# Attention weights turned by two DMA transposes, with the taps laid in another order in PSUM and a new order of issue

## The chip, the cores and the metric

The kernel runs on one core of a Trainium2 chip. The metric is the device time of one execution in microseconds (us), and lower is better. A core has five engines with instruction streams of their own: TensorE (PE in the profile; its weight loads are listed apart as PEld), VectorE (DVE), ScalarE (ACT), GpSimd (POOL) and SyncE (SP), which here only issues DMAs. Matrix products go to PSUM, a small accumulator memory, and are copied from there to SBUF, the main on-chip memory, by DVE or ACT.

## What is computed

Two independent layers on inputs of 2048 positions by 448 features, whose outputs stand side by side in the result. Cut to what matters:

```python
# A: a diagonal state space model with complex state of 448
h = Lam_bar * h + Bu[:, t]                     # for each t of 2048
y = 2.0 * einsum("blp,dp->bld", hseq, Cmat).real + x * Dskip

# B: attention of each position to 8 earlier ones, 2 apart
H, Dh, W, dil = 16, 28, 8, 2
idx = pos[:, None] - (arange(W) * dil)[None, :]
logits = einsum("bhsd,bhswd->bhsw", q, k[idx]) * Dh ** -0.5
logits = where(idx >= 0, logits, -1e9)
attn = softmax(logits, axis=-1)                # over the W = 8 taps
o = einsum("bhsw,bhswd->bhsd", attn, v[idx])
out_b = o.reshape(B, S, D) @ wo

out = concatenate([y, out_b], axis=-1)
```

All inputs and outputs are bf16.

## The kernel before, in words

**Layout.** The 2048 positions are 128 chunks of 16: position = 16 * chunk + j. Keys, queries and values are made for one j at a time, so a tap (2 positions back) is mostly another j of the same chunk, and only the first few j reach into the chunk before, for which small halo copies exist. Attention is worked in two halves, b = 1 (j from 8 to 15) first, then b = 0. In a half, 8 positions j are split as r (2 runs) and i (4 within a run).

**Attention up to the weights (class PartB).** `prep` (L411) makes queries and keys on PE, four chunks' columns at a time (L476, L483, L509), and ACT or DVE copies them out of PSUM. `qk` (L579) multiplies queries and keys of a pair of taps on DVE (L649, L651, L655) into one of three product buffers; `summ` sums the products over Dh on PE (L666, L672) into the PSUM tile `logits` of 128 partitions (i, r, head) by 8 taps by 128 chunks. `softmax` (L689), once for each half, is a chain over engines: the mask is added on PE (`mask`, in `consts2`, L247), DVE takes the maximum over taps (`top`, L695), PE subtracts it (`sub`, L699), ACT takes the exponential (`exp`), PE sums over taps (`tot`, L710), DVE normalizes (`norm`, L714 and L716) into `attn_t`. Now the weights stand as (i, r, head) by chunk, while the values stand by chunk on partitions. So `tr` (L722) turns the eight 128x128 blocks on PE into a PSUM tile, and `ev` (L727) copies them in two pieces on ACT to the tile `attn`, whose free dimensions there are ordered so that two taps of a pair lie next to each other.

**The weighted sum.** `pv` (L788) multiplies weights by values on DVE (`mul`, L817: 3584 elements on each of 128 partitions, two taps at a time, 16 times in all) and adds them (L820, L829, L832). Half and run go in the order (b, r) = (1,1), (1,0), (0,1), (0,0). For three of these four groups the result is turned by a DMA transpose on SP (`trd`, L857); for the last one PE turns it (L869) and ACT copies it (L874). PE multiplies by the output weights (L885, L893, L900), and the result is copied out (L214, L218) and stored by SP (L910).

**The state space model (class PartA)** is interleaved with it: small parameters (L1092 to L1103) and powers of the state matrix (L1182) on DVE, the scan and its products on PE (L1232 to L1339), outputs on PE (L1430, L1434), copied or added (L1446) and stored (L1449). SP loads x by DMA transposes (L979), C by eight DMAs (L1005), and turns C by one more (L1009).

**What sets the order.** Every piece of work is a unit given to `Planner.add` (L115) with its engine (or two to choose from), a planned cost, its dependencies and the buffers that it takes and gives back. `Planner.run` (L129) issues the units in the order of the hand-over list `ORDER` if its length is that of the list of units, which is so here; a number from 1000 on means the unit's second engine (for evictions, DVE in place of ACT). Each engine then does its own instructions in that order, and waits are set by what each reads and writes. All DMAs of SP use eight semaphores in turn, so a DMA waits until the eighth one before it has landed. PSUM tiles come from small pools: the tag "W" has one slot (the logits), "s" six, which `tr`, `tot`, the output products and others share; there are three product buffers.

Of the kernel before, what the change touches and what calls it, by code (L numbers as in the profile page):

```python
# [18 lines left out]
NCH = 128  # L19
# [185 lines left out]
class Ctx:  # L205
# [41 lines left out]
    def consts2(self):  # L247
# [22 lines left out]
        def masks():  # L270
            G.memset(mrow[:], 0.0)
            G.affine_select(out=mrow[:], in_=mrow[:], compare_op=ALU.not_equal, fill=-1e9,
                            base=-3, pattern=[[1, 4]], channel_multiplier=1)
            G.memset(mcol[:], 1.0)
            for b in range(2):
                for k in range(2):
                    v = mcol[:, b, k].rearrange("p (i r h) -> p i r h", i=4, r=2)
                    G.affine_select(out=v, in_=v, compare_op=ALU.is_ge, fill=0.0, base=8 * k - 8 * b - 1,
                                    pattern=[[-1, 4], [-4, 2], [0, H]], channel_multiplier=2)
# [36 lines left out]
class PartB:  # L316
# [262 lines left out]
    def qk(self, b, prio):  # L579
# [8 lines left out]
        for g in (2 * b + 1, 2 * b):  # L588
            par = g - 2 * b
            j0 = 4 * g  # L590
            for tp in (3, 2, 1, 0):
# [65 lines left out]
                def summ(g=g, tp=tp, par=par, ub=ub, head=first):  # L657
# [5 lines left out]
                    zs = slice(H - H * par, 3 * H - H * par)  # L663
                    for kt in range(3):
                        for i in range(4):
                            nc.tensor.matmul(lg[32 * i:32 * i + 32, 2 * tp:2 * tp + 2, :],  # L666
                                             lhsT=cx.Z[:, kt, zs], rhs=pr[:, :, i, kt, :],
                                             start=(new and kt == 0), stop=(kt == 2), skip_group_check=True)
                    if tp < 2:
                        for z, t2 in ((cx.Z[:, 3, zs], tp + 2), (cx.Zh[:, zs], tp)):  # L670
                            for i in range(4):
                                nc.tensor.matmul(lg[32 * i:32 * i + 32, 2 * t2:2 * t2 + 2, :],  # L672
                                                 lhsT=z, rhs=ub["p3"][:, :, i, 0, :],
                                                 start=False, stop=True, skip_group_check=True)
# [14 lines left out]
    def softmax(self, b, prio):  # L689
# [29 lines left out]
        def tr():  # L719
            pt = box["pt"] = self.psum.tile([NCH, W, 2, 4, H], bf16, name="pt_at", tag="s")  # L720
            for w in range(W):
                nc.tensor.transpose(pt[:, w].rearrange("q r i h -> q i r h"), box["a"][:, w, :], cx.ident[:])  # L722

        def ev():
            at = self.attn[b] = pool.tile([NCH, W // 2, 2, 2, 4, H], bf16, name="attn%d" % b)
            for x in range(2):
                nc.scalar.copy(at[:, 2 * x:2 * x + 2].rearrange("q z r y i h -> q y (z r) (i h)"),  # L727
                               box["pt"][:, 4 * x:4 * x + 4].rearrange("q (y z) r i h -> q y (z r) (i h)", y=2))
# [6 lines left out]
        u = P.add("PE", pe(8, 128), tr, [u], -1, acq="s", rel="at")  # L735
        self.u_attn[b] = P.add("ACT", 2 * act(512), ev, [u], -1, rel="s")
# [51 lines left out]
    def pv(self, b, prio, deps):  # L788
# [13 lines left out]
        for r in (1, 0):  # L802
            last = getattr(self, "pv_last", None)
            us = (5, 4, 1, 0)
            for n in range(4):

                def step(n=n, r=r, part=0):
# [4 lines left out]
                    def mul(i):  # L812
                        u = us[i]
                        o = j0 + 4 * r + DIL * u
                        aa = self.attn[b][:, 2 * (u // 4) + u % 2, r].rearrange("q y i h -> q (y i) h").unsqueeze(2).to_broadcast(
# [755 lines left out]
```

## Time and profile before

| | before |
|---|---|
| median of 3 runs | 140.28 us |
| lowest and highest run | 140.21 and 141.18 us |
| span of the profiled execution | 138.7 us |
| median less that span | 1.58 us |
| granted TensorE clock | full speed in all 40 slices |
| instructions in the profile | 2854 |
| SP's DMA queue: share of 16 engines' time | 54.0% |

How to read it: the span is the time from the first to the last instruction of one profiled execution; what lies around it is in the median and not in the profile, so a forecast on the span has 1.58 us added. The page gives for each engine its busy time and share, then the chain that ended last (each piece is followed back to what released it). A timeline row gives the start in us, the busy time of a group of like instructions, the engine, the line of the code, the operation, what it writes and reads, and in square brackets how long the engine had been idle and what released it. "x3" at its end is a count. A row on "SPq" is the time that SP takes to issue a DMA; the landing is given apart, from the start of the issue. Since instructions of an engine overlap a little, the next start can lie before the last end, and the pitch of like instructions is shorter than the busy time of one.

### The profile page before, as it was taken

The page shows a single profiled execution, that of the slowest core. Times are in us where ns is not written, and L with a number is a line of the kernel's source. Part 1 is how long each engine was busy: PE and PEld are TensorE (multiplying, and loading weights), DVE is VectorE, ACT ScalarE, POOL GpSimd, SP SyncE. Part 2 cuts the span into 40 slices and gives each one's busy share as a digit, 9 for nine tenths or more (in the row PEclk, how much of TensorE's full clock was granted, in tenths as well). Part 3 has the DMA queues.
Part 4 walks back from the last instruction along what each step waited for, and adds up shares of the span by engine and source line. Part 5 has one row for each costly group of instructions (what it writes and reads, how often), then busy time and mean ns, then how long its engine had stood idle before and what let it go on. Part 6 is the DMA issues. An engine that isn't in the chain of part 4 may idle for free.

```text
span 138.7 us, 2854 instructions
## 1 busy us (share of the span) xinstructions
PE 131.6 (95%) x1078; PEld 68.5 (49%) x1085; DVE 123.8 (89%) x136; ACT 90.0 (65%) x202; POOL 17.7 (13%) x69
## 2 busy tenths in 40 slices
PE   5999999999999999999999999999999999988990
PEld 1634435444555554756435564545655554534640
DVE  2268999899999999999999999999999999999820
ACT  3464589997563967776685998987637070722671
POOL 7489820028000000000000000000000000000000
PEclk9999999999999999999999999999999999999999
DMA  4979943645653349735898019000000827965774
GB/s 128 266 128 213 173 87 63 160 101 116 80 111 74 82 84 145 140 81 150 230 185 195 0 25 112 0 0 2 5 0 0 183 82 43 213 211 155 234 233 139
DMA packets 39582, 16.05 MB, mean 116 GB/s; under 512 B 31573, under 2 KB 38932, under 8 KB 39569
## 3 DMA queue, kind: packets, MB, share of 16 engines
q1 hardware_dynamic: 39506, 15.87, 54.0%
q8 instruction: 8, 0.13, 0.4%
q14 instruction: 5, 0.04, 0.1%
q10 hardware_dynamic: 63, 0.01, 0.0%
HBM read 4.32 MB, written 3.67 MB: 58 GB/s over the span
## 4 chain that ended last, share of the span: by engine, by line
DVE 35%; PE 31%; SPq 15%; issue 7%; DMA 6%; ACT 3%; DVEq 0%; ACTq 0%
DVE rb L820 13%; DVE prods L817 11%; SPq L361 8%; PE v_ps L762 7%; DVE rb L817 4%; PE qk_ps L476 4%; DMA out_dram<-qk 3%; PE logits L666 3%; PE y_ps L1434 3%; DMA rb<-in_B_x_dram 3%; DVE pw L1182 2%; DVE rb L829 2%; PE wo_ps L900 2%; PE scb L1232 2%; PE scp L1232 2%
## 5 line engine op out<-in xcount | busy, mean ns | idle before, releaser
L817 DVE TENSOR_TENSOR prods<-attn,vd 128x3584 bf16<-128x3584 bf16 x12 | 24.1, 2019 | 0.0
L820 DVE TENSOR_TENSOR rb<-rb,prods 128x3584 bf16<-128x3584 bf16 x11 | 22.2, 2021 | 0.1
L651 DVE TENSOR_TENSOR prods<-qk 128x3072 bf16<-128x3072 bf16 (+1 forms) x15 | 19.1, 1327 | 0.0
L214 ACT CAST qk<-wo_ps 128x448 bf16<-128x448 f32 (+1 forms) x16 | 8.3, 527 | 12.2 <-PE wo_ps L893 7.7
L1434 PE MATMUL y_ps<-Ccat,qk 128*128 128x448 bf16 x60 | 15.1, 352 | 0.1
L476 PE MATMUL qk_ps<-rb 128*128 128x512 bf16 x60 | 14.4, 379 | 0.0
L1434 PE MATMUL y_ps<-Ccat,h 128*128 128x448 bf16 x45 | 11.0, 352 | 0.9 <-ACT qk L214 0.9
L214 ACT CAST vd<-v_ps 128x448 bf16<-128x448 f32 x15 | 7.4, 539 | 5.8 <-PE v_ps L762 4.5
L1232 PE MATMUL scb<-xaT_sb,Bcat 128*128 128x512 bf16 x42 | 10.9, 380 | 0.0
L1232 PEld LDWEIGHTS <-Bcat 128*128 128x128 bf16 x84 | 7.6, 100 | 6.6 <-issue 0.4
L1284 ACT CAST ubuf<-scb 128x64 bf16<-128x64 f32 x35 | 7.1, 218 | 5.6 <-PE scb L1291 3.5
L762 PE MATMUL v_ps<-rb 128*128 128x448 bf16 x48 | 9.9, 353 | 0.0
L655 DVE TENSOR_TENSOR prods<-qk 128x768 bf16<-128x768 bf16 (+3 forms) x18 | 9.1, 569 | 0.3 <-ACT qk L214 0.2
L216 ACT ACTIVATE qk<-qk_ps 64x512 bf16<-64x512 f32 (+1 forms) x15 | 8.9, 599 | 0.6 <-PE qk_ps L509 0.3
L476 PEld LDWEIGHTS <-rb 128*128 128x128 bf16 x60 | 5.6, 98 | 7.1 <-DMA rb<-in_B_wqkv_dram 0.5
L1434 PEld LDWEIGHTS <-qk 128*128 128x128 bf16 x60 | 5.9, 98 | 5.3
L817 DVE TENSOR_TENSOR rb<-attn,vd 128x3584 bf16<-128x3584 bf16 x4 | 8.1, 2022 | 0.1
L893 PE MATMUL wo_ps<-wo_p,rb 128*128 128x448 bf16 x36 | 8.1, 354 | 0.0
L1182 DVE TENSOR_TENSOR pw<-Dm,spair 128x1920 bf16<-128x1920 bf16 x7 | 8.1, 1153 | 0.0
L214 ACT CAST qk<-qk_ps 128x512 bf16<-128x512 f32 (+2 forms) x11 | 6.3, 585 | 2.6 <-PE qk_ps L483 1.1
L1232 PE MATMUL scp<-xaT_sb,Bcat 128*128 128x512 bf16 x30 | 7.8, 380 | 0.0
L666 PE MATMUL logits<-prods,Zsel 128*32 128x256 bf16 x192 | 7.4, 274 | 0.0
(199 smaller groups left out, 261.9 us busy)
## 6 DMA issues: line engine op xcount, KB each, us to landing
out_dram<-qk SPq DMA_DIRECT2D x32, 112.0 KB, 1.8
vd<-vd SPq DMA_DIRECT2D x3, 392.0 KB, 4.7
rb<-in_B_wqkv_dram SPq DMA_DIRECT2D x3, 336.0 KB, 5.0
qk<-in_A_x_dram SPq DMA_DIRECT2D x1, 448.0 KB
ra<-in_A_B_re_dram SPq DMA_DIRECT2D x1, 392.0 KB, 4.3
ra<-in_A_B_im_dram SPq DMA_DIRECT2D x1, 392.0 KB, 5.9
rb<-in_A_C_re_dram SPq DMA_DIRECT2D x4, 98.0 KB, 2.9
rb<-in_A_C_im_dram SPq DMA_DIRECT2D x4, 98.0 KB, 2.8
```

The lines of the kernel that those rows point to most:

```text
L214: nc.scalar.copy(out, in_)
L361: nc.sync.dma_start(self.xT[:, j], bass.AP(x.tensor, x.offset + j * D - DT, [[T * D, NCH], [1, KT * NCH]]), transpose=True)
L476: nc.tensor.matmul(out(n), lhsT=w(n, full, k), rhs=self.xT[:, j:j + 4, k, :], start=(not rfirst and k == 1), stop=(rfirst and k == KT - 1) ...
L651: V.tensor_tensor(out.rearrange("p i j k q -> p i (j k) q"), qq.unsqueeze(1).to_broadcast([NCH, 2, 4 * nk, NCH]), bass.AP(kk.tensor, kk.of ...
L655: V.tensor_tensor(jk(out[:, i, a:e]), qq, kk, op=ALU.mult)
L666: nc.tensor.matmul(lg[32 * i:32 * i + 32, 2 * tp:2 * tp + 2, :], lhsT=cx.Z[:, kt, zs], rhs=pr[:, :, i, kt, :], start=(new and kt == 0), st ...
L762: nc.tensor.matmul(box["ps"][:].rearrange("p h d -> p (h d)"), lhsT=self.xT[:, j, k, :], rhs=self.wv[:, k, :], start=False, stop=(k == KT ...
L817: V.tensor_tensor(tmp[i].rearrange("p (j d h) -> p j d h", j=8, d=DH), aa, self.vd[:, o:o + 8], op=ALU.mult)
L820: V.tensor_tensor(acc, acc, tmp[i], op=ALU.add)
L1182: V.tensor_tensor(t[:], self.o["Dm"][:].rearrange("p (a b) -> p a b", b=2).unsqueeze(1).to_broadcast([NCH, 2 * NPW, 32, 2]), self.sp[:, m ...
L1232: mt(box[i], lhsT=self.Bcat[:, k, m, :], rhs=self.xk(slice(i, None, 4), k), start=(i % 2 == 0 and k == 0), stop=False, **kw)
L1434: nc.tensor.matmul(ps, lhsT=h, rhs=self.Ccat[:, m, :], start=(m == 0 and not skip), stop=(m == NM - 1), skip_group_check=True)
```

## The change

Four things change together.

1. `tr` and `ev` of the softmax, 8 PE transposes and 2 ACT copies for each half, give way to one unit, `turn`: a DMA transpose on SP of `attn_t` (128 partitions by 8 times 128) straight to the tile `attn`, once for each half. The PSUM tile between them is not used any more.
2. A DMA transpose can't reorder what it turns, so the order of taps is set earlier: `summ` writes the two taps of a pair to places two apart in `logits` (two runs of 128 columns for each matmul in place of one of 256), the pattern of the mask row changes with it, and `mul` reads the weights from the new tile: runs of 16 heads, 32 elements apart.
3. `ORDER` is new as a whole. Units have other numbers from the second half of the list on, since two are gone. Among what moves: the first evictions of queries and keys stand in another order, with the small parameter chain of the state space model between them; several evictions change between DVE and ACT; the mask rows stand earlier on POOL; three pairs of halo copies, the three small loads of Dskip and the eight loads of C stand ahead of the first `turn` on SP, and the loads of the output weights behind it; the loads of x and of Dskip for the last step stand earlier.
4. Nothing else: the products, sums, scan and outputs are the same operations in the same numbers.

```diff
 ORDER = [
-    1, 22, 4, 5, 2, 3, 0, 36, 38, 40, 24, 41, 39, 7, 8, 6, 9, 19, 13, 12, 11, 10, 14, 15, 18, 16, 17, 1037, 26, 28,
-    45, 1043, 49, 50, 67, 62, 63, 44, 1042, 30, 1068, 51, 64, 54, 21, 29, 31, 35, 32, 222, 1052, 1066, 55, 1058,
-    1053, 56, 1057, 1065, 1046, 82, 83, 69, 70, 84, 71, 171, 1085, 1072, 59, 60, 61, 74, 75, 76, 87, 73, 78, 79, 88,
-    47, 1086, 1077, 172, 181, 223, 33, 262, 80, 154, 81, 103, 104, 90, 91, 105, 92, 95, 173, 107, 167, 96, 94, 106,
...
-    635, 610, 583, 593, 584, 594, 590, 599, 591, 600, 595, 596, 620, 685, 686, 682, 678, 597, 592, 683, 680, 679,
-    598, 585, 586, 587, 601, 602, 603, 486, 413, 450]
+    1, 3, 4, 2, 0, 36, 38, 22, 21, 24, 5, 39, 8, 40, 6, 1037, 35, 41, 9, 49, 1045, 50, 26, 42, 7, 44, 62, 63,
+    1043, 64, 28, 12, 54, 51, 1052, 55, 65, 56, 29, 53, 19, 11, 10, 1066, 30, 67, 1046, 13, 58, 14, 1068, 69,
+    59, 15, 17, 82, 70, 1057, 60, 83, 1061, 71, 31, 16, 74, 220, 1072, 18, 84, 73, 75, 86, 76, 1085, 171, 87,
+    103, 77, 90, 78, 32, 1047, 108, 88, 104, 20, 91, 172, 79, 154, 80, 105, 174, 92, 81, 1109, 181, 93, 107, 94,
...
+    587, 588, 563, 607, 612, 598, 676, 559, 589, 669, 605, 591, 581, 592, 582, 608, 590, 599, 600, 678, 560,
+    593, 684, 594, 583, 595, 677, 679, 584, 601, 596, 585, 680, 484, 681]
@@ -269,8 +270,9 @@
 
         def masks():
             G.memset(mrow[:], 0.0)
-            G.affine_select(out=mrow[:], in_=mrow[:], compare_op=ALU.not_equal, fill=-1e9,
-                            base=-3, pattern=[[1, 4]], channel_multiplier=1)
+            v = mrow[:].rearrange("p (z y) -> p y z", z=2)
+            G.affine_select(out=v, in_=v, compare_op=ALU.not_equal, fill=-1e9,
+                            base=-3, pattern=[[2, 2], [1, 2]], channel_multiplier=1)
             G.memset(mcol[:], 1.0)
             for b in range(2):
                 for k in range(2):
@@ -661,15 +663,16 @@
                     new = tp // 2 not in begun
                     begun.add(tp // 2)
                     zs = slice(H - H * par, 3 * H - H * par)
+                    at = lambda t, i: lg[32 * i:32 * i + 32, 4 * (t // 2) + t % 2:4 * (t // 2) + t % 2 + 3:2, :]
                     for kt in range(3):
                         for i in range(4):
-                            nc.tensor.matmul(lg[32 * i:32 * i + 32, 2 * tp:2 * tp + 2, :],
+                            nc.tensor.matmul(at(tp, i),
                                              lhsT=cx.Z[:, kt, zs], rhs=pr[:, :, i, kt, :],
                                              start=(new and kt == 0), stop=(kt == 2), skip_group_check=True)
                     if tp < 2:
                         for z, t2 in ((cx.Z[:, 3, zs], tp + 2), (cx.Zh[:, zs], tp)):
                             for i in range(4):
-                                nc.tensor.matmul(lg[32 * i:32 * i + 32, 2 * t2:2 * t2 + 2, :],
+                                nc.tensor.matmul(at(t2, i),
                                                  lhsT=z, rhs=ub["p3"][:, :, i, 0, :],
                                                  start=False, stop=True, skip_group_check=True)
                     cx.pr_ring.put(ub["r"])
@@ -716,24 +719,16 @@
             V.tensor_tensor(box["a"][:].rearrange("p w (c a) -> p w c a", c=2), box["e"][:].rearrange("p w (a c) -> p w c a", c=2),
                             r[:].rearrange("p o (a c) -> p o c a", c=2).to_broadcast([NCH, W, 2, 64]), op=ALU.mult)
 
-        def tr():
-            pt = box["pt"] = self.psum.tile([NCH, W, 2, 4, H], bf16, name="pt_at", tag="s")
-            for w in range(W):
-                nc.tensor.transpose(pt[:, w].rearrange("q r i h -> q i r h"), box["a"][:, w, :], cx.ident[:])
-
-        def ev():
-            at = self.attn[b] = pool.tile([NCH, W // 2, 2, 2, 4, H], bf16, name="attn%d" % b)
-            for x in range(2):
-                nc.scalar.copy(at[:, 2 * x:2 * x + 2].rearrange("q z r y i h -> q y (z r) (i h)"),
-                               box["pt"][:, 4 * x:4 * x + 4].rearrange("q (y z) r i h -> q y (z r) (i h)", y=2))
+        def turn():
+            at = self.attn[b] = pool.tile([NCH, W, 4, 2, H], bf16, name="attn%d" % b)
+            nc.sync.dma_start(at[:].rearrange("q w i r h -> q w (i r h)"), box["a"][:].rearrange("p w q -> p (w q)"), transpose=True)
         u = P.add("PE", 0.07, lambda: cx.mask(b, self.lg[b]), self.u_lg[b] + [cx.u_mask], -1)
         u = P.add("DVE", 1.23, top, [u], prio, acq="mx")
         u = P.add("PE", pe(2, 512), sub, [u], -1, rel="mx")
         u = P.add("ACT", act(1024) + 1.3, exp, [u], -1, rel="W", acq="ex")
         u = P.add("PE", pe(8, 128), tot, [u], -1, acq="s")
         u = P.add("DVE", 2.175, norm, [u], prio, rel=("s", "ex"), acq="at")
-        u = P.add("PE", pe(8, 128), tr, [u], -1, acq="s", rel="at")
-        self.u_attn[b] = P.add("ACT", 2 * act(512), ev, [u], -1, rel="s")
+        self.u_attn[b] = P.add("SP", 1.3, turn, [u], -1, rel="at", lat=3.0)
 
     def v_proj(self, prio, deps):
         nc, pool, P, cx = self.nc, self.pool, self.plan, self.cx
@@ -812,7 +807,8 @@
                     def mul(i):
                         u = us[i]
                         o = j0 + 4 * r + DIL * u
-                        aa = self.attn[b][:, 2 * (u // 4) + u % 2, r].rearrange("q y i h -> q (y i) h").unsqueeze(2).to_broadcast(
+                        w0 = 4 * (u // 4) + 2 * (u % 2)
+                        aa = self.attn[b][:, w0:w0 + 2, :, r, :].rearrange("q y i h -> q (y i) h").unsqueeze(2).to_broadcast(
                             [NCH, 8, DH, H])
                         V.tensor_tensor(tmp[i].rearrange("p (j d h) -> p j d h", j=8, d=DH), aa, self.vd[:, o:o + 8], op=ALU.mult)
 
```

51 rows, old and new, of the table ORDER are left out of this document.

## The prediction

> **What bounds the kernel now.** I read the page first (busy shares), then the chain of waits in order of time, then the timelines of DVE, PE and SP.
>
> ```profile
> PE 131.6 (95%) x1078; PEld 68.5 (49%) x1085; DVE 123.8 (89%) x136; ACT 90.0 (65%) x202; POOL 17.7 (13%) x69
> ```
>
> ```profile
> 22.58 1.29 PE qk_ps L476 x6
> ...
> 56.33 0.45 PE pt_at L722 x8
> ...
> 59.84 0.83 DVE prods L655 x3
> ...
> 113.66 1.10 DVE rb L829
> ...
> 124.01 0.31 issue
> 124.32 0.92 ACT qk L214
> 125.28 2.81 PE y_ps L1434 x14
> ```
>
> TensorE (PE) is busy 95% of a 138.7 us span and VectorE (DVE) 89%. The chain runs through both in turn: PE in the first part (22.58, 56.33), DVE from 59.84 to 113.66, PE again from 125.28. Neither has slack: what is saved on PE counts only where DVE doesn't arrive later than PE does. PE runs 512 columns in 0.215 us (six in 1.29), and its one sizeable idle stretch late in the run ends at 125.28, where ACT had taken 0.92 us for an eviction. Everything that PE still waits for I put at about 2 us. So DVE's order of arrival decides, and I follow it through four points.
>
> ```profile
> 7.02 0.23 DVE L218 COPY rb<-rb 64x256 bf16<-64x256 bf16 x1 [0.78 <-DMA rb<-in_B_wqkv_dram]
> 8.07 0.29 DVE L218 COPY wm<-rb 128x512 bf16<-128x512 bf16 x1 [0.82 <-DMA rb<-in_B_wqkv_dram]
> 8.28 0.25 DVE L1092 TENSOR_TENSOR den<-pf 128x7 f32<-128x7 f32 x1
> ...
> 9.84 0.68 DVE L220 TENSOR_SCALAR qk<-qk_ps 128x512 bf16<-128x512 f32 x1
> ...
> 18.62 1.83 DVE L649 TENSOR_TENSOR prods<-qk 128x1536 bf16<-128x1536 bf16 x2
> 20.37 1.15 DVE L1182 TENSOR_TENSOR pw<-Dm,spair 128x1920 bf16<-128x1920 bf16 x1
> 21.43 0.62 DVE L1130 TENSOR_TENSOR Gd<-Dm,gs 128x896 bf16<-128x896 bf16 x1
> ...
> 30.37 1.90 DVE L655 TENSOR_TENSOR prods<-qk 128x768 bf16<-128x768 bf16 x3 [0.20 <-ACT qk L214]
> ...
> 43.41 1.22 DVE L695 TENSOR_REDUCE mx<-logits 128x128 bf16<-128x1024 f32 x1
> 44.56 0.61 DVE L218 CAST vd<-v_ps 128x448 bf16<-128x448 f32 x1
> ...
> 63.37 1.22 DVE L695 TENSOR_REDUCE mx<-logits 128x128 bf16<-128x1024 f32 x1
> 64.51 2.02 DVE L817 TENSOR_TENSOR rb<-attn,vd 128x3584 bf16<-128x3584 bf16 x1
> ...
> 82.67 1.23 DVE L716 TENSOR_TENSOR attn_t<-ex_sb,rsum 128x1024 bf16<-128x1024 bf16 x1
> ...
> 99.86 2.03 DVE L817 TENSOR_TENSOR rb<-attn,vd 128x3584 bf16<-128x3584 bf16 x1
> ...
> 126.52 2.10 DVE L832 TENSOR_TENSOR rb<-rb,prods 128x1792 bf16<-128x1792 bf16 x2
> 128.53 1.08 DVE L1411 TENSOR_TENSOR qk<-qk,rb 128x1792 bf16<-128x1792 bf16 x1
> ```
>
> The points: the big products start at 30.37, the first softmax's maximum at 43.41, the second's at 63.37, and the last addition of the weighted values ends at 128.53. From there 10.2 us remain to 138.7. From 18.62 on DVE has hardly a pause, so a late start is carried to the end.
>
> **The change part by part.** The profiled span is 138.7 us and the median 140.28, so 1.58 us lie around the span; I sum on the span.
>
> *TensorE's transposes and ACT's copies go.* Two halves of 8 transposes, 0.45 us each by the chain: PE loses 0.9 us of work. ACT loses four copies:
>
> ```profile
> L727 ACT COPY attn<-pt_at x4: 592/599/606, 57.0 to 87.9; 128x512 bf16<-128x512 bf16 x4
> ```
>
> That is 2.4 us, off the path: the first pair is done by 58.1 and its reader starts at 64.51; the second by 88.5, its reader at 99.86. Taking PE's part out is worth 0.9 us only if PE sets the end; where DVE does, it is worth nothing. I take 0, with −0.9 as the other end.
>
> *Two DMA transposes come, on SP's queue.* Nearest rows are the transposes of the weighted values (L857, 128x1792) and of C (L1009); the turned tile is 128x1024.
>
> ```profile
> L857 SPq DMA_TRANSPOSE rb<-rb x3: 1518/1540/1558, 81.6 to 114.8; - x3
> ...
> DMA to landing us min/median/max: 4.0/4.0/4.0
> ```
>
> ```profile
> L1009 SPq DMA_TRANSPOSE Ccat<-rb x1: 4297/4297/4297, 68.5 to 68.5; - x1
> ...
> DMA to landing us min/median/max: 6.0/6.0/6.0
> ```
>
> ```profile
> 48.08 1.27 SPq L979 DMA_TRANSPOSE xaT_sb<-in_A_x_dram  x1
> 49.45 2.72 SPq L1005 DMA_DIRECT2D rb<-in_A_C_re_dram  x4
> 52.22 2.72 SPq L1005 DMA_DIRECT2D rb<-in_A_C_im_dram  x4
> 54.98 5.37 SPq L401 DMA_DIRECT2D wo_p<-in_B_wo_dram  x8
> 60.46 0.58 SPq L775 DMA_DIRECT2D vd<-vd  x1
> 61.08 0.98 SPq L776 DMA_DIRECT2D vd<-vd  x1
> ```
>
> I take 4.0 us, the row nearest in size and with SBUF on both sides, and keep 6.0. SP issues in order. In the changed order the x loads end as now (49.35); then come three pairs of halo copies (1.6 the pair above, so up to 4.8), three small skip loads (each like the 0.58 row, 1.5) and the eight C loads (5.5), and only then the first turn: issue at 60.6–61.2, landing at 64.6–65.2, or 67.2 with 6.0. Its reader, the first weighted product, comes 1.15 us behind the second maximum, so at 64.5 if nothing else moves and near 66 by the sum below. So the wait is 0–2 us; I take 0.2, since at 4.0 us the landing lies ahead of a lagging DVE. What stands behind the turn on SP is the transpose of C, the last halo pair and the loads of the output weights. The output weights now come after it, about 5.5 us later than their 60.4 today, and are first needed after the first DVE transpose at 81.6, so they stay hidden. The second turn hangs on the normalization, which in the order stands three weighted products and more ahead of its reader as it does now (82.67 to 99.86): hidden by some 10 us, even at 6.0.
>
> The Trainium skill, Advanced Engine Details and Errata, section X-Bar Transpose (TRN2), says that transposing DMAs run as fast as ordinary ones, at 350–400 GB/s, while DMA: Bandwidth & Descriptors, Latency and other measured facts, has 261 GB/s for one with a strided middle dimension. The turned tile of 262 KB would by that move in an estimated 0.7–1.0 us beside a fixed part, and land sooner than my 4.0, so the term of 0.2 would be 0. The rows here bear the faster page out only in part: the transpose of C takes 6.0 us.
>
> *Taps laid in another order.* The summing matmuls write two runs of 128 columns apart instead of one of 256, same columns. The weighted product (L817) now reads runs of 16 elements 32 apart, not 16. L1182 already reads operands in short runs and makes 1920 elements in 1.15 us (0.60 ns each) beside L817's 3584 in 2.02 (0.56): no price for either. Were L817 at one element per 0.96 ns, 1.7 times as slow, 16 of them would cost 22 us; I give that under 2 in 100, since its innermost runs stay whole.
>
> *Order of DVE's opening.* Now the first projection starts on PE at 6.82:
>
> ```profile
> 6.82 1.47 PE L476 MATMUL qk_ps<-rb 128*128 128x512 bf16 x6
> 8.13 1.03 PE L509 MATMUL qk_ps<-rb 128*128 128x512 bf16 x4
> ```
>
> The changed order has DVE's first eviction wait for sixteen matmuls of 0.215 us (twelve L476, then L483): 10.3 plus a release, 10.5 in all, against 9.84. DVE stands idle before it, since the chain of small operations that starts at 8.28 and ends at 9.84 (1.55 us) now follows two evictions. From 10.5 to the big products DVE then has: 12 evictions of about 0.64 (pitch of the 0.68 rows; two of the 14 now made have gone to ACT, net) = 7.7; the small chain 1.55; three copies of 0.29 = 0.9; two edge copies 0.4; six half products of 0.9 = 5.4; L1130 0.54; three L1182 of 1.07 = 3.2. That is 19.7, and with the waits of today's stretch (1.2–1.9) the big products start at 31.4–32.1, not 30.37: a lag of 1.0–1.7. I take 1.35. It is none if the order closes those waits; then it is −0.2 (19.7 + 10.5 = 30.2).
>
> *Other engines.* The swap of evictions leaves ACT at 65% less the four copies; two K evictions that it takes over stand ahead of the big products, whose first row already waited 0.20 for ACT, so they are part of the lag and no term of their own. POOL, busy 17.7 us, gets the mask rows earlier, with another pattern and the same count: nothing, since it has 87% of the span idle.
>
> *From there to the second maximum.* The product work is the same. One eviction of V (0.61 at 44.56) goes to ACT: −0.55. The third product buffer is now asked for before PE has summed an earlier one: 0–0.9, I take 0.45. The mask's matmuls, put on PE just ahead of the first maximum, can be queued behind one or two groups of PE's other work there: 0–0.35, I take 0.2. Sum so far +1.45, second maximum near 64.8.
>
> *Weighted values.* Same operations in the same numbers: 63.37 to 128.53 is 65.2 us and stays so. With the 0.2 of the turn: +1.65, the last addition ends near 130.2.
>
> *Tail.*
>
> ```profile
> 128.50 1.49 PE L1434 MATMUL y_ps<-Ccat,S 128*128 128x448 bf16 x7
> 129.82 1.50 PE L869 MATMUL pt_o<-ident,rb 128*128 128x128 bf16 x24
> ...
> 132.72 2.43 PE L900 MATMUL wo_ps<-wo_p,rb 128*128 128x448 bf16 x12
> ```
>
> Now 10.2 us: PE still owed other matmuls when the last half addition came. In the changed order PE does in the tail four groups of 8 transposes (0.45 each), four output groups (0.76 each) and two groups of y (1.3–1.4): 7.6–7.9, then 0.3 for the eviction and 2.4 or so to the end as now: 10.6. I take +0.4, between −0.9 (PE less backlogged) and +0.8.
>
> Sum: 1.35 − 0.55 + 0.45 + 0.2 + 0.2 + 0.4 = +2.05 on 138.7 gives 140.75, with 1.58 around it 142.3 us.
>
> **The rivals.** *A, PE sets the end (faster).* If the opening's lag doesn't arise (big products start by 30.4), DVE is 0.5 us earlier by the evicted V, and PE's 0.9 us come through together with up to 0.9 of the stall ahead of 125.28: 140.28 − 0.9 to −1.8 = 138.5–139.4. For it: PE at 95%, and a chain that has PE in its last 13 us. Against it: DVE's list in the opening, which is longer than what fits. The point that decides is a start of the big products at 30.4 or sooner.
>
> *B, the first turn comes late.* If the eight C loads hold it and it lands after 6.0, DVE stands 1–2 us before the first weighted product, with all 65 us of DVE work behind it. By that 143.3–144.3. For it: SP's order; against it: L857's 4.0.
>
> *C, no measurable change.* The lag is half as large, since today's waits in the stretch are filled by the moved evictions (+0.5), and the terms of buffer and mask are 0 with the tail as now: 138.7 + 0.5 − 0.55 to + 1.2 gives 140.2–141.5.
>
> **How the numbers follow.** Chances: my sum with its own range 141.7–143.2, 0.40; B 0.10; C 0.28; A 0.20; the slow reading of L817 0.02. The time is the first's, 142.3. The range goes from 139.4 (the slow end of A) to 144.0 (most of B), which leaves out about 2 in 10. One per cent, 138.88 to 141.68, is about what a measurement here can tell from no change. Faster by more: most of A, 0.17. Within: C and the slow end of A, 0.31. Slower: 0.52.
>
> **What would show it.** In the changed profile: no matmul into the transposed attention on PE and no copy of it on ACT (−0.9 and −2.4 of busy time); a landing of about 4 us for both turns; L817 still at 2.02; DVE's first eviction at 10.5 and the big products at 31.4–32.1; the second maximum near 64.8 and a wait ahead of the first weighted product of under 1 us, its releaser the turn's DMA if B holds; the last addition near 130.2. The forecast is wrong if the big products start before 30.5, or if DVE ends its additions before 128.5.

## The result and the profile after

The changed kernel takes 144.43 us (median of 4 runs, 143.32 to 144.78) where the kernel before takes 140.26; the ratio is 1.0257, with a 95% interval of 1.0207 to 1.0308. Measured a second time, on the chip of later experiments, it took 143.04 us, ratio 1.0228 [1.0180, 1.0276]. Two of the first four runs, 144.71 and 144.78, had a granted clock of 0.988 and lie 1.4 us above the lowest, which lifts the first median. So the kernel is slower by 2 to 3%, the way that was forecast: 142.3 was some 1.6 us too low, and the first median lies 0.4 above the end of the range while 140.28 times the ratio, 143.9, lies just within it. The profiled execution took 143.32 us with a span of 141.6, 2.9 more than the 138.7 of before.

The page of the changed kernel: busy times, then the 40 slices of TensorE (PE).

```profile
PE 132.1 (93%) x1063; PEld 67.8 (48%) x1069; DVE 122.6 (87%) x134; ACT 89.8 (63%) x200; POOL 19.0 (13%) x69
...
PE   5999999999999999999999899999999999893990
```

PE's busy time is no smaller than the 131.6 of before, but it says little about the 16 transposes that are gone: both profiles lack a few matmuls (1063 are listed beside 1069 weight loads here, 1078 beside 1085 before). Near the end there is a slice with a 3: PE stood idle there.

The timeline of VectorE (DVE) in the changed kernel, at the points that the forecast followed (start, busy time, what; in brackets the idle time before and its releaser):

```profile
10.86 0.69 DVE L219 CAST qk<-qk_ps 128x512 bf16<-128x512 f32 x1 [3.58 <-PE qk_ps L485]
...
31.93 1.90 DVE L657 TENSOR_TENSOR prods<-qk 128x768 bf16<-128x768 bf16 x3 [0.27 <-ACT qk L215]
...
43.65 1.76 DVE L653 TENSOR_TENSOR prods<-qk 128x3072 bf16<-128x3072 bf16 x1 [0.52 <-PE logits L669]
45.34 1.23 DVE L698 TENSOR_REDUCE mx<-logits 128x128 bf16<-128x1024 f32 x1
...
51.80 3.43 DVE L653 TENSOR_TENSOR prods<-qk 128x3072 bf16<-128x3072 bf16 x2 [0.76 <-PE logits L669]
...
65.59 1.23 DVE L698 TENSOR_REDUCE mx<-logits 128x128 bf16<-128x1024 f32 x1
66.86 2.03 DVE L813 TENSOR_TENSOR rb<-attn,vd 128x3584 bf16<-128x3584 bf16 x1
...
128.71 2.09 DVE L828 TENSOR_TENSOR rb<-rb,prods 128x1792 bf16<-128x1792 bf16 x2
...
138.20 0.62 DVE L1442 TENSOR_TENSOR qk<-y_ps,qk 128x448 bf16<-128x448 f32 x1 [1.27 <-PE y_ps L1430]
```

Beside the rows of before: the big products start 1.56 us later (31.93 for 30.37), the first maximum 1.93 (45.34 for 43.41), the second 2.22 (65.59 for 63.37), the last additions end 2.2 later (130.8 for 128.6), and the end stands 10.8 us behind them in place of 10.1. The lag grows in steps, two of them waits for PE (0.52 and 0.76), and then stays the same for 65 us.

The first turn in the changed kernel, from the rows of its line and of SP's queue:

```profile
L724 SPq DMA_TRANSPOSE attn<-attn_t x2: 1233/1275/1317, 63.5 to 91.1; - x2
...
DMA to landing us min/median/max: 3.2/3.2/3.2
```

```profile
56.74 3.03 SPq L1001 DMA_DIRECT2D rb<-in_A_C_re_dram  x4
59.82 3.62 SPq L1001 DMA_DIRECT2D rb<-in_A_C_im_dram  x4
63.54 1.32 SPq L724 DMA_TRANSPOSE attn<-attn_t  x1
```

It is issued behind C's loads at 63.54, some 2.5 later than I had counted, and lands after 3.2, not 4.0: at 66.7. DVE's second maximum ends at 66.82 and its first weighted product starts at 66.86. That is 1.27 us behind the start of the maximum, where it was 1.14 before, so the turn costs 0.1 us at most. It is a close thing: in this execution it would have come late for a DVE on time, while in a second profile of the same kernel it is issued at 61.62.

The end of PE's timeline in the changed kernel:

```profile
126.68 1.49 PE L1430 MATMUL y_ps<-Ccat,S 128*128 128x448 bf16 x7
129.86 0.51 PE L865 MATMUL pt_o<-ident,rb 128*128 128x128 bf16 x6 [1.70 <-DVE rb L828]
130.87 0.29 PE L865 MATMUL pt_o<-ident,rb 128*128 128x128 bf16 x2 [0.49 <-DVE rb L828]
130.99 0.73 PE L1430 MATMUL y_ps<-Ccat,h 128*128 128x448 bf16 x3
131.56 0.92 PE L1430 MATMUL y_ps<-Ccat,qk 128*128 128x448 bf16 x4
...
136.68 0.73 PE L1430 MATMUL y_ps<-Ccat,h 128*128 128x448 bf16 x3
137.25 0.92 PE L1430 MATMUL y_ps<-Ccat,qk 128*128 128x448 bf16 x4
```

PE waits 1.70 and 0.49 us for DVE's last additions, while two output groups of the state space model (1.3 us each, 130.99 and 136.68) stand behind the first or the last of the transposes in its order. In the kernel before, the same stretch has no such wait: PE still owed other work when the additions came.

### The profile page after: what moved, and what is told of

It reads as the page before. It is cut to its first block, busy times and chain, and to the rows that moved or that the text cites. A ratio compares the mean times of both kernels' runs of the same rounds, so it can differ in the third digit from the quotient of the medians.

```text
span 141.6 us, 2836 instructions
## 1 busy us (share of the span) xinstructions
PE 132.1 (93%) x1063; PEld 67.8 (48%) x1069; DVE 122.6 (87%) x134; ACT 89.8 (63%) x200; POOL 19.0 (13%) x69
## 4 chain that ended last, share of the span: by engine, by line
DVE 51%; PE 34%; issue 6%; ACT 5%; DMA 2%; DVEq 0%
DVE rb L816 15%; DVE prods L813 15%; PE qk_ps L478 8%; PE v_ps L757 7%; DVE rb L813 6%; DVE prods L653 4%; ACT qk L215 3%; PE qk_ps L511 2%; DVE pw L1178 2%; PE logits L669 2%; PE wo_ps L896 2%; DMA ra<-in_B_x_dram 2%; PE y_ps L1430 2%; PE qk_ps L485 2%; PE scp L1228 2%
## 5 line engine op out<-in xcount | busy, mean ns | idle before, releaser
L478 PE MATMUL qk_ps<-rb 128*128 128x512 bf16 x60 | 15.0, 380 | 0.2 <-ACT Bcat L215 0.2
L215 ACT CAST vd<-v_ps 128x448 bf16<-128x448 f32 x16 | 8.0, 534 | 5.9 <-PE v_ps L757 5.8
L215 ACT CAST qk<-qk_ps 128x512 bf16<-128x512 f32 (+2 forms) x16 | 9.3, 585 | 2.3 <-PE qk_ps L485 1.2
L215 ACT CAST qk<-y_ps 128x448 bf16<-128x448 f32 (+1 forms) x9 | 5.8, 668 | 6.9 <-PE y_ps L1430 6.1
L757 PE MATMUL v_ps<-rb 128*128 128x448 bf16 x48 | 10.1, 353 | 0.0
L217 ACT ACTIVATE qk<-qk_ps 128x512 bf16<-128x512 f32 (+1 forms) x14 | 8.1, 592 | 1.9 <-PE qk_ps L485 1.8
```

The lines of the kernel that those rows point to most:

```text
L215: nc.scalar.copy(out, in_)
L217: nc.scalar.mul(out, in_, scale)
L478: nc.tensor.matmul(out(n), lhsT=w(n, full, k), rhs=self.xT[:, j:j + 4, k, :], start=(not rfirst and k == 1), stop=(rfirst and k == KT - 1) ...
L757: nc.tensor.matmul(box["ps"][:].rearrange("p h d -> p (h d)"), lhsT=self.xT[:, j, k, :], rhs=self.wv[:, k, :], start=False, stop=(k == KT ...
```

## The experiments

My theory: the two DMA turns are worth about nothing, and the new order of issue is what costs, in the opening and in the tail. Rival one: the turns and the layout cost. Rival two: not DVE's list in the opening but PE and ACT make the lag. Every kernel was run beside the kernel before; ratios are to it. "Old order" is the order of the kernel before with the units renumbered for the changed kernel. The code's line numbers shift by up to 6 with the change and the length of the list.

**Old order with the DMA turns.**

```diff
-ORDER = [new order]
+ORDER = [old order; C's loads and then the first turn where TensorE's first turning stood]
```

> The changed kernel with the order of issue of the kernel before: the taps' new layout and both DMA turns stay, the written order is the old one with the units renumbered; the first turn and the eight loads of C stand on SP where TensorE's first turning stood, C ahead. Theory (the new order is what costs): the two turns are worth between 0 and the 0.9 us of TensorE work that goes, so 139.4 to 140.3 us, ratio to before 0.993 to 1.000. Rival one (the turns and the new layout cost, through SP's queue, strided writes to PSUM or a late first turn): 142 us or more, ratio 1.012 and up.

Measured: 139.77 us, ratio 0.9999 [0.9962, 1.0036]. Span, busy times and the shares of the chain that ended last, and DVE's timeline:

```profile
span 138.5 us, 2830 instructions
...
PE 131.8 (95%) x1069; PEld 67.9 (49%) x1069; DVE 124.2 (90%) x136; ACT 88.3 (64%) x198; POOL 17.3 (13%) x69
...
PE 89%; DMA 6%; ACT 2%; issue 1%
```

```profile
126.91 2.09 DVE L826 TENSOR_TENSOR rb<-rb,prods 128x1792 bf16<-128x1792 bf16 x2
```

Rival one falls: turns and layout together make no difference beyond the interval of 0.4%. Why the 0.9 us of PE work bring no gain stays open. The chain that ended last is PE for 89% of the span, so one would expect them back. The busy time (131.8 for 131.6) doesn't settle it, since the profile of the kernel before lacks seven of its 1085 matmuls.

**New order with TensorE's turns.**

```diff
 # the kernel before
-ORDER = [old order]
+ORDER = [new order; tr and ev some 1 us behind each normalization, in place of turn]
```

> The kernel before with the new order: TensorE turns the weights (8 transposes) and ACT copies them for each half, put some 1 us behind the normalization in the new order; taps as before. Theory (the new order costs, the turns are worth about nothing): 143.2 to 145 us, ratio 1.02 to 1.035, the second maximum near 65.6 and the end 10.5 us or more behind the last addition. Rival one (the turns by DMA cost): under 141.5 us, ratio under 1.01.

Measured: 145.11 us, ratio 1.0330 [1.0293, 1.0368]. The order costs without the turns too. It is 0.7 to 1.0% more than with them, but that is partly my placing of the transposes: ACT's two copies now stand ahead of a small copy that PE waits 1.28 us for, and DVE's second maximum, expected near 65.6, comes at 67.72. (An earlier placing, directly behind each normalization, made the engines wait for one another without end, so that kernel has no time.)

```profile
67.72 1.23 DVE L694 TENSOR_REDUCE mx<-logits 128x128 bf16<-128x1024 f32 x1 [1.90 <-PE logits L284]
```

**The small chain early.**

```diff
-    ... 1043, 64, 28, 12, 54, 51, 1052, ... 1066, 30, 67, ...
+    ... 1043, 64, 30, 28, 12, 54, 51, 1052, ... 1066, 67, ...
```

> The changed kernel with one unit moved: the small parameter chain on DVE (1.5 us) stands ahead of DVE's first eviction, where DVE was idle from 7.3 to 10.9. Theory as in the prediction (DVE's list in the opening makes the lag): the big products start at 30.4 to 30.8 in place of 31.9 and the second maximum at 64.1 to 64.6 in place of 65.6; the first weighted product stays near 66.8, because the first turn lands at 66.7 by SP's queue, so the time moves by less than 0.5 us from the changed kernel. Rival two (not DVE's list but TensorE and ACT's evictions, through which the chain that ended last runs from 7 to 52 us): the big products start at 31.5 or later and the second maximum stays within 0.4 of 65.6.

Measured: 143.2 us, ratio 1.0267 [1.0200, 1.0335]: no gain. DVE's timeline in it:

```profile
13.04 0.69 DVE L219 TENSOR_SCALAR qk<-qk_ps 128x512 bf16<-128x512 f32 x1 [0.59 <-PE qk_ps L509]
...
15.95 0.69 DVE L217 CAST qk<-qk_ps 128x512 bf16<-128x512 f32 x1 [0.90 <-PE qk_ps L483]
...
31.52 1.90 DVE L655 TENSOR_TENSOR prods<-qk 128x768 bf16<-128x768 bf16 x3 [0.27 <-ACT qk L213]
```

The chain's 1.5 us are gone from DVE's list and come back as waits for PE (0.59, 0.90 and smaller ones). The big products start at 31.52, and seven profiles of kernels whose opening is the unchanged new one have 31.34 to 31.98: no gain that can be told from chance. The second maximum stays within 0.4 of the changed kernel's (65.19 for 65.59). So DVE's list is not what makes the opening late, and rival two fits, since the waits are for PE. Which piece of PE's or ACT's order does it, this run doesn't show.

**The tail refilled.**

```diff
-    ... 682, 656, 586, 670, 675, ... 676, 559, ... 677, 679, ... 681, 680, 484, 681]
+    ... 682, 675, 679, 656, 586, 670, ... 676, 680, 559, ... 677, 681, ... 484]
```

> The changed kernel with the last two output groups of the state space model (positions 13 and 14, 2.7 us of TensorE) put ahead of the last transposes, in the 1.7 and 0.5 us in which TensorE waits for DVE's last additions, and the copy and store of position 14 moved with them. Theory (the order of the tail gives 2 us away): 1.3 to 2.2 us less than the changed kernel, 142 to 143 us, ratio 1.012 to 1.02 to before, with the end 8.5 to 9.3 us behind the last addition in place of 10.8. Against it: no change over 0.5 us if the last copies or stores set the end.

Measured: 142.32 us, ratio 1.0192 [1.0132, 1.0252]; the end stands 10.1 us behind the last addition, where 8.5 to 9.3 was expected, and the time is 0.7 us below the second measurement of the changed kernel, where 1.3 to 2.2 was. PE's timeline in it:

```profile
130.40 1.06 PE L863 MATMUL pt_o<-ident,rb 128*128 128x128 bf16 x16
132.44 0.92 PE L894 MATMUL wo_ps<-wo_p,rb 128*128 128x448 bf16 x4 [0.98 <-DVE qk L1440]
133.97 1.05 PE L863 MATMUL pt_o<-ident,rb 128*128 128x128 bf16 x16 [0.61 <-DVE qk L1440]
```

The wait ahead of the transposes is gone, and 0.98 and 0.61 us of others come: the two groups now hold PSUM slots until DVE, busy with the additions, copies them out (L1440). Here the filled gap is paid for with slots. This run also shows the first turn late by a little, since DVE's second maximum comes 0.6 us sooner (65.00):

```profile
66.62 2.03 DVE L811 TENSOR_TENSOR rb<-attn,vd 128x3584 bf16<-128x3584 bf16 x1 [0.39 <-DMA attn<-attn_t]
```

**The old opening, the rest new; and its complement.** Split at the first maximum.

```diff
-ORDER = [new order]
+ORDER = [old order up to the first maximum] + [what is left, in the new order]
```

> The changed kernel, with all units that the old order has ahead of the first maximum in the old order and on the old engines, the rest in the new order. Theory (about 1.9 of the 2.9 us are lost in the opening, the rest in the tail): first maximum at 43.4 to 43.7, second at 63.6 to 64.3, 141.0 to 142.4 us, ratio 1.008 to 1.017; within this the first turn may hold the first weighted product by up to 1 us, since SP issues it behind C's loads. If the loss lay behind the first maximum: 143 us or more, ratio over 1.02.

Measured: 143.62 us, ratio 1.0206 [1.0155, 1.0258], which is what was expected of a loss behind the first maximum. DVE in it, and then PE:

```profile
44.00 1.23 DVE L696 TENSOR_REDUCE mx<-logits 128x128 bf16<-128x1024 f32 x1
...
52.22 3.43 DVE L651 TENSOR_TENSOR prods<-qk 128x3072 bf16<-128x3072 bf16 x2 [2.53 <-ACT xaT_sb L213]
```

```profile
51.59 0.84 PE L667 MATMUL logits<-prods,Zsel 128*32 128x256 bf16 x24 [1.19 <-ACT ex_sb L706]
```

The first maximum comes 1.3 us sooner than in the changed kernel, and 2.53 us of waiting behind it use that up: the second maximum stands at 66.0. The sums that would free DVE's product buffer wait 1.19 us on PE for the first exponential, which still reads the one slot of the logits. The two orders don't fit at the seam, so the run doesn't price the opening; it does show that a DVE that is sooner at the first maximum isn't a faster kernel with the new rest.

```diff
-ORDER = [new order]
+ORDER = [new order up to the first maximum] + [what is left, in the old order]
```

> The complement: the changed kernel with the new order ahead of the first maximum, and all that is left in the old order. Theory: the lag of the opening is carried to the end and the old tail gives 0.5 to 1 us back: first maximum at 45.0 to 45.4, last addition at 130 to 130.9, 141.4 to 142.6 us, ratio 1.010 to 1.018. If the opening's lag is made up on the way: under 140.6 us, ratio under 1.005.

Measured: 141.93 us, ratio 1.0122 [1.0082, 1.0163]. Here too the seam costs a wait (1.30 us ahead of the normalization), and the last additions end at 131.1, later than in the changed kernel. Yet the end is 1.3 us sooner, 9.2 us behind them in place of 10.8. That pointed to the tail.

**The turn ahead of C's loads**, in the kernel with the old opening:

```diff
-    ... 528, ... 152, ... 211, ... 212, ...
+    ... 528, ... 211, ... 212, 152, ...
```

> As the kernel with the old opening and the new rest, and on SP the first turn stands ahead of the eight loads of C. If the first turn holds the first weighted product there (rival B of the prediction, hidden in the changed kernel only because DVE comes late): the wait goes and the time falls by as much, 0.3 to 1.0 us. If it doesn't: the same within 0.4 us, or slower by up to 1 us where C's later transpose holds TensorE.

Measured: 143.47 us, ratio 1.0219 [1.0185, 1.0252], the same. With a DVE as late as this (second maximum at 66.02) the turn's place on SP has no weight (rival B of the prediction); what it would cost a DVE on time, this run can't show.

**The exponential ahead**, once alone and once with the turn ahead of C's loads too.

```diff
-    ... 511, 512, 501, 143, 513, 261, 514, 130, 150, 502, 208, 149, 503, 209, 222, ...
+    ... 511, 512, 501, 143, 513, 130, 208, 261, 149, 503, 209, 514, 502, 150, 222, ...
```

> The changed kernel with the first softmax's subtraction on TensorE put ahead of one group of the state model's sums, and its exponential on ACT ahead of two copies of V and one of x. Theory (behind the first maximum it is the late exponential, which frees the one PSUM slot of the logits, that makes DVE wait 0.76 us for a product buffer): exponential at 47.6 to 48.6 in place of 50.1, that wait under 0.2, second maximum at 64.7 to 65.0; the first weighted product then waits for the first turn (releaser: its DMA) and starts at 66.4 to 66.9 as before, so the time stays within 0.5 us of the changed kernel. If the wait comes from elsewhere (TensorE's length of work): second maximum within 0.2 of 65.6.

Measured: 144.47 us, ratio 1.0312 [1.0264, 1.0360], 1.4 us above the changed kernel beside it where at most 0.5 was expected; the second maximum stands at 65.89. The exponentials, and then DVE and PE behind the first one:

```profile
L706 ACT ACTIVATE ex_sb<-logits x2: 1024/1046/1068, 48.6 to 68.0; 128x1024 bf16<-128x1024 f32 x2
```

```profile
52.09 3.43 DVE L651 TENSOR_TENSOR prods<-qk 128x3072 bf16<-128x3072 bf16 x2 [1.31 <-ACT vd L213]
```

```profile
50.08 1.46 PE L1226 MATMUL scp<-xaT_sb,Bcat 128*128 128x512 bf16 x6 [0.43 <-ACT vd L213]
51.46 0.84 PE L667 MATMUL logits<-prods,Zsel 128*32 128x256 bf16 x24
```

The exponential does start 1.5 us sooner, at 48.6, and DVE's wait grows from 0.76 to 1.31. The sums that free the product buffer come behind six of the state model's in PE's order, and those now wait 0.43 for the copies of V that I moved back on ACT. So the exponential alone doesn't make the wait. In the changed kernel it ends at 51.11 and the sums start at 51.17, straight behind the same six: two conditions are met at once there, and moving one leaves the other, PE's list.

```diff
+    ... 211, ... 212, 152, ...   # and the same moves as above
```

> The same, with the first turn ahead of C's eight loads on SP. Theory: the first turn lands by 64, the first weighted product starts at 65.8 to 66.2 with no wait for a DMA, the last addition ends 0.6 to 1.0 us sooner than in the changed kernel, and the time falls by 0.5 to 1.0 us. If the turn's place is without weight: as the kernel before it, within 0.2 us.

Measured: 145.03 us, ratio 1.0333 [1.0279, 1.0386]; second maximum at 66.2, 65.9 without it. No gain from the turn's place either, with DVE this late.

**The old tail, and the new tail alone.** Split at the second step of the last weighted group (unit 576).

```diff
-ORDER = [new order]
+ORDER = [new order up to the last group's second step] + [what is left, in the old order]
```

> The changed kernel up to the last group of weighted products (its second step), all that is left then in the old order. Theory (the order of the tail leaves TensorE idle for 2.2 us ahead of the last additions, with 2.7 us of output work behind them): no such idle time, the end 9.2 to 9.9 us behind the last addition in place of 10.8, 0.9 to 1.6 us less than the changed kernel, ratio 1.010 to 1.019. If the lateness of DVE alone makes the end: as the changed kernel within 0.4 us.

> The changed kernel as it is, beside the next three on the same chip: 143.3 to 144.8 us, ratio 1.02 to 1.03; the last addition near 130.8 and the end 10.8 us behind it.

Measured: the old tail 140.54 us, ratio 1.0036 [1.0006, 1.0066], better than expected, beside the changed kernel's 1.0228 on the same chip. The last additions of the changed kernel in this measurement, then DVE and PE of the kernel with the old tail:

```profile
128.33 2.09 DVE L828 TENSOR_TENSOR rb<-rb,prods 128x1792 bf16<-128x1792 bf16 x2
```

```profile
65.26 1.23 DVE L696 TENSOR_REDUCE mx<-logits 128x128 bf16<-128x1024 f32 x1
...
128.24 2.09 DVE L826 TENSOR_TENSOR rb<-rb,prods 128x1792 bf16<-128x1792 bf16 x2
```

```profile
127.77 0.73 PE L887 MATMUL wo_ps<-wo_p,rb 128*128 128x448 bf16 x3
128.34 1.49 PE L1428 MATMUL y_ps<-Ccat,S 128*128 128x448 bf16 x7
129.66 0.50 PE L863 MATMUL pt_o<-ident,rb 128*128 128x128 bf16 x6
130.39 1.18 PE L863 MATMUL pt_o<-ident,rb 128*128 128x128 bf16 x18 [0.23 <-DVE rb L826]
...
132.65 2.43 PE L894 MATMUL wo_ps<-wo_p,rb 128*128 128x448 bf16 x12
```

DVE is as late as in the changed kernel (65.26, and 130.3 at the last addition), and the end still comes 8.3 us behind it, at 138.6. PE waits 0.23, not 2.2, since the output groups come ahead of the transposes, and nothing but the last products stands behind them.

```diff
-ORDER = [new order]
+ORDER = [the same units up to there in the old order] + [what is left, in the new order]
```

> The complement of the kernel with the old tail: the changed kernel with the same units up to the last group of weighted products in the old order and on the old engines, and only what is left then in the new order. DVE should be on time: last addition at 128.6 to 129.3. Theory (the new tail needs 10.5 us or more behind the last addition whenever that comes, the old one 8.3 to 9.8): end 10.3 to 11 us behind it, 140.8 to 142 us, ratio 1.004 to 1.013, with TensorE idle for over 1 us ahead of the last transposes. If the new tail costs only when DVE is late: the end 9.8 us or less behind the last addition, ratio under 1.002.

Measured: 141.75 us, ratio 1.0076 [1.0044, 1.0107]. DVE and PE in it:

```profile
127.02 2.09 DVE L826 TENSOR_TENSOR rb<-rb,prods 128x1792 bf16<-128x1792 bf16 x2
```

```profile
129.17 0.29 PE L863 MATMUL pt_o<-ident,rb 128*128 128x128 bf16 x2 [0.24 <-DVE rb L826]
129.29 0.73 PE L1428 MATMUL y_ps<-Ccat,h 128*128 128x448 bf16 x3
...
134.98 0.73 PE L1428 MATMUL y_ps<-Ccat,h 128*128 128x448 bf16 x3
135.55 0.92 PE L1428 MATMUL y_ps<-Ccat,qk 128*128 128x448 bf16 x4
```

With DVE on time (129.1) PE hardly waits (0.24; the expected hole of over 1 us is not there), but the two output groups still stand behind the transposes, and the end is 10.8 us behind the last addition. The four corners, all with the DMA turns:

| order up to the last group | old tail | new tail | last addition | end behind it, old and new tail |
|---|---|---|---|---|
| old | 0.9999 | 1.0076 | 129.0, 129.1 | 9.5, 10.8 |
| new | 1.0036 | 1.0228 | 130.3, 130.4 | 8.3, 10.8 |

The late DVE alone costs 0.4%, the new tail alone 0.8%, both 2.3%. That is 1.2% more than their sum, with an uncertainty of some 0.7% from the four intervals. The old tail gives 1.2 us back to a late DVE, since PE owes other work then; the new one gives nothing back. No run was faster than both kernels by more than its interval.

## Why the prediction was right, and where it was not

- **TensorE's 0.9 us and ACT's 2.4, taken as 0:** right. With the old order the ratio is 0.9999, so rival A (PE sets the end, and its 0.9 us come through) didn't come, though the opening's lag is gone there and the chain is nearly all PE. Why not stays open.
- **The turns:** the sum had 0.2 us for the first; it was 0.1 at most, and by luck. The turn landed at 66.7, not at 64.6 to 65.2: issued some 2.5 us later on SP than counted, landed 0.8 sooner. It stayed hidden only because DVE's second maximum was 0.8 later than forecast too. With that at 64.8 the product would by estimate (64.8 + 1.15 against 66.7) have waited some 0.8 us, as it did 0.39 in the run with the refilled tail. The Trainium skill, DMA: Bandwidth & Descriptors, section Anatomy of one DMA, gives a fixed part of about 2.0 us for a DMA on GpSimd's path; with 262 KB at the 261 GB/s quoted in the prediction that makes an estimated 3.0 us, close to the 3.2 here, for a DMA of SP. The second turn was hidden, as said: issued at 91.1, read at 102.06.
- **Layout:** right. Weighted products take 2.02 to 2.03 us as before, and the changed matmuls into PSUM keep their mean of 274 ns. No row shows the 0.96 ns per element of the slow reading; the products take 0.56. No run tries a DMA transpose that reorders, so that the taps had to be laid anew isn't shown.
- **Opening, +1.35:** 1.56 measured, first eviction at 10.86 for 10.5. The size was right, by luck, since the reason was wrong: I had it in DVE's list, with the small chain behind two evictions. Taking the chain out of that list gained nothing that can be told from chance, its time turning into waits for PE. In which piece of PE's and ACT's new order the lag lies is not settled; the two runs split at the first maximum made waits of their own at the seam.
- **Waits behind it:** 0.45 for a product buffer; two waits, 0.52 and 0.76, came. The term was too small by 0.8, about as much as the second maximum was later than forecast (65.6 for 64.8). The 0.2 for the mask shows nowhere: no wait is listed ahead of either maximum.
- **Weighted values unchanged:** right, 65.2 us from the second maximum to the last addition in both.
- **Tail, +0.4:** by this sum +0.7 (10.8 for 10.1). With the new tail the late start is indeed carried to the end, which stands 10.8 us behind the last addition with DVE late or on time. What failed is the step in its general form, "a late start is carried to the end", with the tail's change a small term beside it. It is carried to the last addition and no further if PE has other work then: with the old tail a DVE that is 1.7 us late (130.3 for 128.6) ends at 138.6, 0.1 us sooner than the kernel before. So most of the 2.9 us needs the new tail as it meets a late DVE. The sum came out near because it put the whole lateness on DVE and priced the tail against the on-time kernel, whose reserve ("PE still owed other matmuls") it noted and didn't count.
- **Clock:** it has no term in the sum. Of the changed kernel's first four runs two have a span of 143.0 and 143.1 at a granted clock of 0.988, one 142.4 at 1.0, and the profiled one 141.6 at 0.996. The first two are 1.4 to 1.5 us above the span that the steps here are measured on. The profile of the run with the small chain early has that clock too (0.988) and shows where the time goes: the clock is at 0.56 from 131 to 134 us, right behind PE's wait for the last additions. Three matmuls of an output group take 1.33 us there, for 0.73, and the end is 12.3 us behind the last addition, for 10.8. The run with the exponential ahead has that clock in three of its six runs and the one after it in four, which lifts their medians. What makes the 142.4 stays open.

## What to carry to other kernels

Where two engines are both near full, ask at the end of the program which of them still owes work when the last result of the other arrives: a lag costs little while there is such work (0.4% here), and all of itself once the order has put that work elsewhere. Price the order of the tail with the lateness that the change itself makes, not with the times of the kernel before. And a list that is too long on one engine is only the cause if taking an entry out moves the end: here the entry's time came back as a wait for another engine.

## What the runs showed of the hardware

- A DMA transpose of 128x1024 bf16 from SBUF to SBUF lands after 3.1 to 4.2 us in these runs (3.2 in the changed kernel), while SP spends 1.23 to 1.48 us on its issue.
- Six of the kernels here (the changed one among them) show PE waiting 2.1 to 2.2 us ahead of the last transposes. Of their 40 runs 14 have a mean granted clock of 0.983 to 0.988; in all other kernels, where that wait is 1.2 us or less, none of 115 runs is below 0.994. That the wait brings the clock down was not tested.
